# When an evicted PSUM bank counts as free, and which banks the expert layers may use, in a planned attention-and-expert kernel

## The chip, the cores and the metric

One core of one Trainium2 chip runs the program. The metric is the device time of one execution in microseconds, the median over several runs. Profiles come from single executions of the same program; their times are given in microseconds from the start of the span, the first to the last instruction on the core.

## What is computed

Sliding-window causal attention (8 batches, 8 heads, 576 tokens, head size 64, window 64), and behind it one feed-forward expert on all 4608 tokens:

```python
scores = (1 / sqrt(64)) * q @ k.T            # per batch and head
mask = (rel >= 0) & (rel < 64)               # rel = query position - key position
attn = softmax(where(mask, scores, -1e9))
x = (attn @ v) -> [4608, 512]                # heads side by side
h = x @ w_in                                 # 512 -> 2048
g = h * sigmoid(h)                           # silu
out = g @ w_out                              # 2048 -> 512
```

Inputs and outputs are float32; the kernel computes its matmuls in bfloat16 and accumulates in float32.

## The kernel before

**Two kinds of work share TensorE.** *Attention* goes batch by batch. A batch is three units of 192 query tokens. A unit (`add_unit`, from line 486) is one scores step of 48 small matmuls (L331) into four PSUM banks, four exponentials on ScalarE (L337), four mask products on VectorE (L340), one values step of 48 small matmuls (L349) into two banks, and for each of these a reciprocal (L356), a normalisation (L359) and a transpose (L363) into the SBUF tensor `bridge`, which holds the attention output for the expert.

*The expert* (`add_tile`, from line 531) goes over nine tiles of 512 tokens, numbered 0 to 8. The first layer of a tile is 16 groups, one for each 128 hidden columns. A group is four matmuls of 512 columns (L369) that accumulate in one bank; ScalarE evicts the bank with silu into an SBUF tile `g` (L375). The second layer is four output groups of 128 tokens; each is 16 matmuls of 512 columns (L381) into one bank, which ScalarE or VectorE copies to SBUF (L387), and SP stores to HBM (L391). Tiles 0 and 1 are cut into narrower pieces, since their input is only just there; in the last tile the last output group is cut into 256, 128 and 128 columns.

**Eight banks, three pools.** A PSUM bank holds 512 float32 numbers on each partition, one group. Line 177 names the pools: `at`, banks 0 to 3, for scores; `pv`, banks 4 and 5, for values; `mp`, banks 4 to 7, for the expert; and `all`. So values and expert share banks 4 and 5.

**The order is planned ahead.** `Plan.run` (lines 47 to 119) is a list scheduler that runs while the program is built. Every operation has a class, a duration for each engine that can do it, dependencies, a class rank and a *lat*. The planner steps through modelled time and gives each free engine the ready operation of the lowest rank; expert matmuls have rank 99, so attention goes first when it can. Classes are first in, first out, so the expert's matmuls keep their order, and scores may start only while more than 14 second-layer matmuls of the tile are left (`scores_may_run`, line 402). The result is a fixed instruction order for each engine. On the chip the engines wait for each other by semaphores; modelled times have no force there, only the order and the banks.

**When a bank is free, for the planner.** An operation is *seen* at its modelled end plus its *lat* (line 97). A bank is given until an operation that frees it (`untils`): the silu (line 563) or the copy (line 584), and for values the normalisation. It is idle once that operation has been seen (line 75). Among the idle banks, line 80 sorts: for the expert, banks 6 and 7 come ahead of 4 and 5, and within each pair the one seen longest ago. The default *lat* is 0.08 us (line 28). A first-layer matmul is modelled at 0.0036 + columns/2400 us, with *lat* 0.1 (line 555); a silu at 0.18 + columns × 0.00083 us (line 561), and 1.28 more where ScalarE's function table changes (line 93); a copy at 0.18 + columns/1160 us on ScalarE (line 581).

Of the kernel before, what the change touches and what calls it, by code (L numbers as in the profile page):

```python
# [14 lines left out]
class Plan:  # L15
# [31 lines left out]
    def run(self):  # L47
        head = {c: 0 for c in self.queues}
        engines = sorted({e for q in self.queues.values() for op in q for e in op["us"]})
        free = {e: 0.0 for e in engines}  # L50
        can = {e: [c for c, q in self.queues.items() if any(e in op["us"] for op in q)] for e in engines}
        table, left = "exp", self.count
        pipe, sent = {True: 2.0, False: 0.0}, []
        events, order = [0.0], []
        while left:
            if not events:
                raise RuntimeError([(c, head[c], q[head[c]]["n"]) for c, q in self.queues.items() if head[c] < len(q)])
            now = self.now = heapq.heappop(events)
            while events and events[0] == now:
                heapq.heappop(events)  # L60
            moved = True
            while moved:
                moved = False
                for e in engines:
                    if free[e] > now:
                        continue
                    best, kept = None, set()
                    heads = [(self.queues[c][head[c]], c) for c in can[e] if head[c] < len(self.queues[c])]
                    for op, c in sorted(heads, key=lambda x: x[0]["first"]):
                        if e == "POOL" and op["dma"] and len(sent) >= 8 and sent[-8] > now:  # L70
                            continue
                        if e not in op["us"] or not self.done(op["deps"]) or (op["gate"] and not op["gate"]()):
                            continue
                        if op["pool"]:
                            idle = [i for i in self.pools[op["pool"]] if i not in kept and self.done(self.banks[i])]
                            if len(idle) < len(op["untils"]):
                                if op["pool"] != "mp":
                                    kept.update(self.pools[op["pool"]])
                                continue
                            idle.sort(key=lambda i: (op["pool"] == "mp" and i in self.pools["pv"],  # L80
                                                     max([u["seen"] for u in self.banks[i]], default=0.0)))
                            op["bank"] = idle[:len(op["untils"])]
                            for i, until in zip(op["bank"], op["untils"]):
                                self.banks[i] = until
                        best = (op, c)
                        break
                    if best is None:
                        continue
                    op, c = best
                    head[c] += 1  # L90
                    us = op["us"][e]
                    if op["table"] and op["table"] != table:
                        table, us = op["table"], us + 1.28
                    end = free[e] = now + us
                    soft = e == "POOL"
                    if op["dma"] is None:
                        op["seen"] = end + op["lat"]
                    elif soft:

                        begin = max(pipe[True], end + 1.4)  # L100
                        pipe[True] = begin + op["dma"] * (1.5 if pipe[False] > begin else 1.0)
                        op["seen"] = pipe[True] + op["lat"] + 1.2
                        sent.append(op["seen"])
                        heapq.heappush(events, op["seen"])
                    else:
                        begin = max(pipe[False], end + 1.0)
                        busy = pipe[True] > begin
                        pipe[False] = begin + op["dma"] * (1.6 if busy else 1.0)
                        if busy:
                            pipe[True] += 0.6 * op["dma"]  # L110
                        op["seen"] = pipe[False] + {"ld0": 1.2, "st": 1.2}.get(c, 3.0)
                    op["at"], op["cls"], op["by"] = now, c, e
                    order.append((op, e))
                    left -= c != "warm"
                    moved = True
                    heapq.heappush(events, end)
                    heapq.heappush(events, op["seen"])
        for op, e in order:
            op["fn"](e)
# [3 lines left out]
def kernel(ctx, tc, q, k, v, w_in, w_out, out):  # L123
# [244 lines left out]
    def first_layer(bank, j, ft, c, lo, hi):  # L368
        nc.tensor.matmul(  # L369
            banks[bank["bank"][0]][:, 0:hi - lo], lhsT=w_in_sb[:, c, ft * 128:(ft + 1) * 128],  # L370
            rhs=bridge[:, (j * TT + lo) // 64:(j * TT + hi) // 64, c], start=(c == 0), stop=(c == NDC - 1),
        )

    def silu(bank, gt, lo, hi):
        nc.scalar.activation(out=gts[gt][:, lo:hi], in_=banks[bank["bank"][0]][:, 0:hi - lo], func=ACTF.Silu)  # L375
# [4 lines left out]
    def second_layer(bank, gt, m, f, lo, hi):  # L380
        nc.tensor.matmul(  # L381
            banks[bank["bank"][0]][:, 0:hi - lo], lhsT=gts[gt][:, m * 128:(m + 1) * 128], rhs=w_out_sb[:, f, lo:hi],
            start=(f == 0), stop=(f == NFT - 1),
        )

    def copy_out(e, bank, ot, lo, hi):
        copies[e](out=ots[ot][:, lo:hi], in_=banks[bank["bank"][0]][:, 0:hi - lo])  # L387

    def store(ot, j, m, lo, hi):
        r0 = j * TT + m * 128  # L390
        nc.sync.dma_start(out=out[r0:r0 + 128, lo:hi], in_=ots[ot][:, lo:hi])  # L391
# [134 lines left out]
    n_gt, free_gt = [0], {}  # L526
    n_ot, free_ot = [0], {}
# [3 lines left out]
    def add_tile(j):  # L531
# [18 lines left out]
        for i, (ft, lo, hi) in enumerate(work):  # L550
            have = [op for n in range((j * TT + hi + 191) // 192) for op in o_done[n]]
            g, si = gt[ft]
            bank = None
            for c in range(NDC):
                op = p.add("moe", {"PE": 0.0036 + (hi - lo) / 2400}, None,
                           have + win[ft] + (exps[0] if j == 0 else []), lat=0.1,
                           pool=None if c else "mp")
                bank = bank or op
                op["fn"] = lambda _, bank=bank, ft=ft, c=c, lo=lo, hi=hi: first_layer(bank, j, ft, c, lo, hi)
                moe.append((op, 1, 1 if c == 0 and (i == 0 or hi > work[i - 1][2]) else -1))  # L560
            si.append(p.add("silu", {"ACT": 0.18 + (hi - lo) * 0.00083}, lambda _, bank=bank, g=g, lo=lo, hi=hi:
                            silu(bank, g, lo, hi), [op] + free_gt.get(g, []), table="silu"))
            bank["untils"][0] = [si[-1]]
        order = [(m, f, 0, d_model) for m in range(4) for f in range(NFT)]
        if j == 0:
# [3 lines left out]
        bank, uses = {}, {}  # L569
        for i, (m, f, lo, hi) in enumerate(order):  # L570
            g = gt[f][0]
            op = p.add("moe", {"PE": 0.0036 + (hi - lo) / 2400}, None, gt[f][1] + [wout[f // 2]], lat=0.1,
                       pool=None if f else "mp")
            bank.setdefault((m, lo), op)
            op["fn"] = lambda _, bank=bank[(m, lo)], g=g, m=m, f=f, lo=lo, hi=hi: second_layer(bank, g, m, f, lo, hi)
            moe.append((op, 2, len(order) - i))
            uses.setdefault(g, []).append(op)
            if f == NFT - 1:
                ot = n_ot[0] % NOT
                n_ot[0] += 1  # L580
                cp = p.add("out", {"DVE": 0.18 + (hi - lo) / 1000, "ACT": 0.18 + (hi - lo) / 1160},
                           lambda e, bank=bank[(m, lo)], ot=ot, lo=lo, hi=hi: copy_out(e, bank, ot, lo, hi),
                           [op, free_ot.get(ot)])
                bank[(m, lo)]["untils"][0] = [cp]
                free_ot[ot] = p.add("st", {"SP": 0.45}, lambda _, ot=ot, m=m, lo=lo, hi=hi: store(ot, j, m, lo, hi), [cp],
                                    dma=0.75 * (hi - lo) / d_model)
# [7 lines left out]
    def warm(op):  # L594
# [4 lines left out]
                 pool="all")  # L599
    for lo, hi in ((0, 256), (256, 512), (512, 1024), (1024, 1536), (1536, 2048)):  # L600
# [6 lines left out]
          table="silu")  # L607
# [10 lines left out]
    while n_tile < NTT:  # L618
        add_tile(n_tile)
        n_tile += 1  # L620
# [31 lines left out]
```

The softmax here doesn't subtract the row's maximum and nothing guards it: scores larger than these inputs give would overflow.

## Time and profile before

| | |
|---|---|
| median of 5 runs | 299.74 us (299.14 to 301.05) |
| the profiled execution, its own time | 301.05 us |
| its span | 299.2 us |
| expert tiles 2 to 6, with attention in them, each | about 31.2 us |
| tile 7 (240.6 to 268.4), no attention | 27.8 us |
| TensorE / ScalarE / VectorE busy | 96% / 59% / 47% |
| evictions by silu, 512 columns | 0.60 us each |
| copies of an output group, 512 columns | 0.58 us each |
| granted clock of TensorE | full, in all slices |
| last loads from HBM issued | 145.0 to 149.0 us |

The first 84 us hold the loads' start, the first two batches of attention, and tiles 0 and 1. From there the program is regular: a tile's first layer in one stretch, then its second layer with the next batch's three units inside it. The last values step is at 238 us; tiles 7 and 8 run without attention.

How to read it: a matmul's record covers its way through the array, and the next matmul starts before it ends. So a TensorE busy share near 100% does not tell whether matmuls follow each other as densely as they can; the distance between the starts of successive ones does. A weight load (PEld) stands beside each matmul and overlaps it. A row's idle is the time in which that engine did nothing just before it, and behind the arrow stands what released it; "issue" means that the profile shows nothing it waited for.

### The profile page before, as it was taken

The page shows a single profiled execution, that of the slowest core. Times are in us where ns is not written, and L with a number is a line of the kernel's source. Part 1 is how long each engine was busy: PE and PEld are TensorE (multiplying, and loading weights), DVE is VectorE, ACT ScalarE, POOL GpSimd, SP SyncE. Part 2 cuts the span into 40 slices and gives each one's busy share as a digit, 9 for nine tenths or more (in the row PEclk, how much of TensorE's full clock was granted, in tenths as well). Part 3 has the DMA queues.
Part 4 walks back from the last instruction along what each step waited for, and adds up shares of the span by engine and source line. Part 5 has one row for each costly group of instructions (what it writes and reads, how often), then busy time and mean ns, then how long its engine had stood idle before and what let it go on. Part 6 is the DMA issues. An engine that isn't in the chain of part 4 may idle for free.

```text
span 299.2 us, 8484 instructions
## 1 busy us (share of the span) xinstructions
PE 287.0 (96%) x3609; PEld 149.6 (50%) x3641; DVE 139.3 (47%) x340; ACT 176.2 (59%) x340; POOL 117.8 (39%) x175
## 2 busy tenths in 40 slices
PE   8979979899999999999999999999999999999996
PEld 4657634785544544445444544445444544444444
DVE  3882367978886379327941693067006510000000
ACT  4878645886466745675378437752866376126511
POOL 8965995969898989960500000000000000000000
PEclk9999999999999999999999999999999999999999
DMA  8999999999999999992770210011001100110012
GB/s 169 172 175 168 141 169 173 228 142 132 173 172 143 101 180 184 151 100 74 77 75 0 72 39 36 2 37 72 35 0 39 72 35 0 37 71 35 2 70 71
DMA packets 82982, 28.64 MB, mean 96 GB/s; under 512 B 72448, under 2 KB 78208, under 8 KB 82944
## 3 DMA queue, kind: packets, MB, share of 16 engines
q0 software_dynamic: 77184, 18.07, 65.2%
q1 hardware_dynamic: 5760, 10.03, 9.5%
q8 instruction: 28, 0.46, 0.6%
q14 instruction: 10, 0.08, 0.1%
HBM read 36.70 MB, written 9.44 MB: 154 GB/s over the span
## 4 chain that ended last, share of the span: by engine, by line
PE 80%; DMA 8%; POOL 7%; issue 3%; ACT 1%; POOLq 0%; ACTq 0%
PE mp L381 38%; PE mp L369 37%; DMA nat<-in_q_dram 3%; PE mp L349 3%; PE at L331 3%; DMA w_out_sb<-in_moe_w_out_dram 2%; DMA vv<-in_v_dram 2%; POOL vv L253 2%; POOL nat L239 2%; POOL w_out_sb L265 1%; POOL natb L229 1%; POOL w_in_sb L259 1%; ACT ot L387 0%; ACT g L375 0%; PE at L349 0%
## 5 line engine op out<-in xcount | busy, mean ns | idle before, releaser
L369 PE MATMUL mp<-bridge,w_in_sb 128*128 128x512 bf16 (+5 forms) x696 | 128.6, 342 | 2.6 <-ACT g L375 0.8
L381 PE MATMUL mp<-w_out_sb,g 128*128 128x512 bf16 (+2 forms) x576 | 124.4, 367 | 4.5 <-issue 3.2
L375 ACT ACTIVATE g<-mp 128x512 bf16<-128x512 f32 (+5 forms) x174 | 89.6, 523 | 31.4 <-PE mp L369 29.3
L369 PEld LDWEIGHTS <-w_in_sb 128*128 128x128 bf16 x696 | 66.2, 97 | 63.0 <-issue 7.5
L381 PEld LDWEIGHTS <-g 128*128 128x128 bf16 x608 | 56.0, 98 | 62.0 <-issue 1.4
L387 ACT COPY ot<-mp 128x512 f32<-128x512 f32 (+2 forms) x36 | 20.2, 563 | 62.4 <-PE mp L381 43.1
L340 DVE TENSOR_TENSOR e<-e,mask 128x384 bf16<-128x384 bf16 x84 | 26.1, 349 | 49.2 <-ACT e L337 48.7
L337 ACT ACTIVATE e<-at 128x384 bf16<-128x384 f32 x90 | 37.4, 498 | 17.5 <-PE at L331 17.3
L239 POOL DMA_DIRECT2D nat<-in_k_dram x56 | 34.9, 637 | 12.3 <-DMA vv<-in_v_dram 4.3
L253 POOL DMA_DIRECT2D vv<-in_v_dram x32 | 31.9, 1015 | 13.5 <-PE mp L349 12.9
L239 POOL DMA_DIRECT2D nat<-in_q_dram x56 | 34.8, 641 | 3.0 <-DMA w_in_sb<-in_moe_w_in_dram 1.4
L363 DVE STREAM_TRANSPOSE bridge<-ox 128x384 bf16<-128x384 bf16 x48 | 24.8, 553 | 0.0
L246 DVE STREAM_TRANSPOSE qt<-nat 128x576 bf16<-128x576 bf16 x28 | 20.8, 784 | 6.6 <-DMA nat<-in_q_dram 6.6
L246 DVE STREAM_TRANSPOSE kt<-nat 128x576 bf16<-128x576 bf16 x28 | 20.6, 778 | 4.8 <-DMA nat<-in_k_dram 4.8
L359 DVE TENSOR_TENSOR ox<-mp,rc 128x384 bf16<-128x384 f32 x43 | 21.4, 537 | 0.1
L356 DVE RECIPROCAL rc<-mp 128x6 f32<-128x6 f32 x43 | 7.9, 190 | 18.8 <-PE mp L349 18.0
L349 PEld LDWEIGHTS <-e 128*32 128x32 bf16 x1152 | 10.9, 95 | 8.9 <-issue 5.2
L299 DVE COPY vv<-vv 64x576 bf16<-64x576 bf16 (+1 forms) x14 | 7.5, 533 | 13.0 <-DMA vv<-in_v_dram 10.7
L331 PE MATMUL at<-qt,kt 32*128 32x64 bf16 x1008 | 11.9, 190 | 1.0 <-DVE kt L246 1.0
L349 PE MATMUL mp<-vv,e 128*32 128x65 bf16 x1032 | 12.6, 194 | 0.2 <-ACT e L337 0.2
L331 PEld LDWEIGHTS <-kt 32*128 32x128 bf16 x1008 | 9.4, 92 | 5.5 <-issue 3.8
L375 ACT ACT_TABLE_LOAD x7 | 9.0, 1283 | 0.1
(53 smaller groups left out, 85.9 us busy)
## 6 DMA issues: line engine op xcount, KB each, us to landing
out_dram<-ot SPq DMA_DIRECT2D x35, 256.0 KB, 2.1
vv<-in_v_dram POOLq DMA_DIRECT2D x32, 144.0 KB, 5.5
nat<-in_q_dram POOLq DMA_DIRECT2D x56, 72.0 KB, 4.2
nat<-in_k_dram POOLq DMA_DIRECT2D x56, 72.0 KB, 3.9
w_out_sb<-in_moe_w_out_dram POOLq DMA_DIRECT2D x8, 256.0 KB, 6.3
w_in_sb<-in_moe_w_in_dram POOLq DMA_DIRECT2D x6, 256.0 KB, 7.4
w_in_sb<-in_moe_w_in_dram POOLq DMA_DIRECT2D x4, 128.0 KB, 5.4
natb<-in_q_dram POOLq DMA_DIRECT2D x3, 144.0 KB, 4.9
```

Source lines behind the costliest of these rows:

```text
L239: nc.gpsimd.dma_start(out=nats[i][32 * h:32 * h + 32].rearrange("p (m x) -> p m x", m=NB), in_=(q, k)[kk][b, 4 * a + h].rearrange("(m p r) ...
L246: nc.vector.transpose(out=to[:, (2 * a + part) * S:(2 * a + part + 1) * S].rearrange("x (m t r) -> x m r t", t=32, r=2), in_=nats[i].rearr ...
L253: queue[e].dma_start(out=vv[b % NV][:, 2 * g0 + 1:2 * g1 + 1:2, 0:D], in_=v[b].rearrange("h s d -> (h s) d").rearrange("(g p) d -> p g d", ...
L331: nc.tensor.matmul(at_six(op["bank"][h])[:, a, x], lhsT=kt[b % NK][r, at:at + 128], rhs=qt[b % NK][r, at:at + 64], start=(s == a == x == 0 ...
L337: nc.scalar.activation(out=es[n % NE], in_=at_six(bank), func=ACTF.Exp, scale=scale)
L340: nc.vector.tensor_mul(es[n % NE], es[n % NE], mask0 if g == 0 else mask)
L349: nc.tensor.matmul(at_pv(bank)[32 * h:32 * h + 32, x, t], lhsT=e_of(b, a, n, h)[:, x, 32 * t:32 * t + 32], rhs=vv[b % NV][:, (4 * a + h) * ...
L359: nc.vector.tensor_mul(oxs[n % NOX], at_pv(bank)[:, :, :, 0:D], rcs[n % NRC].unsqueeze(3).to_broadcast([128, 3, 2, D]))
L363: nc.vector.transpose(out=bridge[:, n0:n0 + 3, 2 * a:2 * a + 2].rearrange("x t s (u i) -> x t s u i", u=2), in_=oxs[n % NOX].rearrange("p ...
L369: nc.tensor.matmul(banks[bank["bank"][0]][:, 0:hi - lo], lhsT=w_in_sb[:, c, ft * 128:(ft + 1) * 128], rhs=bridge[:, (j * TT + lo) // 64:(j ...
L375: nc.scalar.activation(out=gts[gt][:, lo:hi], in_=banks[bank["bank"][0]][:, 0:hi - lo], func=ACTF.Silu)
L381: nc.tensor.matmul(banks[bank["bank"][0]][:, 0:hi - lo], lhsT=gts[gt][:, m * 128:(m + 1) * 128], rhs=w_out_sb[:, f, lo:hi], start=(f == 0) ...
```

## The change

Two edits in the planner's input, one in its choice of banks.

1. The silu operations and the copies of tiles 2 to 8 (`j > 1`) get *lat* 0.22 in place of 0.08. For the planner their banks come free 0.14 us later, and so do the results that other operations wait for: `g` for the second layer, `ot` for the store.
2. Once the planner has placed the last values step (the queue `pv` is used up), an operation that asks for a bank gets any of the eight in place of its own pool. Only expert groups are left by then. The sort of line 80 stays, so banks 4 and 5 still come last.

No instruction is added or taken away by these lines; what can differ is the bank that a group gets, and through the modelled times the order in which the planner places operations.

```diff
-                            idle = [i for i in self.pools[op["pool"]] if i not in kept and self.done(self.banks[i])]
+                            idle = [i for i in self.pools[op["pool"] if head["pv"] < len(self.queues["pv"]) else "all"] if i not in kept and self.done(self.banks[i])]
                             if len(idle) < len(op["untils"]):
                                 if op["pool"] != "mp":
                                     kept.update(self.pools[op["pool"]])
...
             si.append(p.add("silu", {"ACT": 0.18 + (hi - lo) * 0.00083}, lambda _, bank=bank, g=g, lo=lo, hi=hi:
-                            silu(bank, g, lo, hi), [op] + free_gt.get(g, []), table="silu"))
+                            silu(bank, g, lo, hi), [op] + free_gt.get(g, []), lat=0.22 if j > 1 else 0.08, table="silu"))
             bank["untils"][0] = [si[-1]]
...
                            lambda e, bank=bank[(m, lo)], ot=ot, lo=lo, hi=hi: copy_out(e, bank, ot, lo, hi),
-                           [op, free_ot.get(ot)])
+                           [op, free_ot.get(ot)], lat=0.22 if j > 1 else 0.08)
                 bank[(m, lo)]["untils"][0] = [cp]
```

## The prediction

> **What bounds the kernel now.** I read the page's busy times first, then the groups by line, the chain that ended last, the waits of TensorE after the loads are through, and last the order of time inside one expert tile.
>
> The page:
>
> ```profile
> span 299.2 us, 8484 instructions
> ...
> PE 287.0 (96%) x3609; PEld 149.6 (50%) x3641; DVE 139.3 (47%) x340; ACT 176.2 (59%) x340; POOL 117.8 (39%) x175
> ...
> PEclk9999999999999999999999999999999999999999
> ...
> L369 PE MATMUL mp<-bridge,w_in_sb 128*128 128x512 bf16 (+5 forms) x696 | 128.6, 342 | 2.6 <-ACT g L375 0.8
> L381 PE MATMUL mp<-w_out_sb,g 128*128 128x512 bf16 (+2 forms) x576 | 124.4, 367 | 4.5 <-issue 3.2
> L375 ACT ACTIVATE g<-mp 128x512 bf16<-128x512 f32 (+5 forms) x174 | 89.6, 523 | 31.4 <-PE mp L369 29.3
> ```
>
> TensorE is busy 96% of the span and no other engine passes 59%; the granted clock is full in all 40 slices. The two expert layers, L369 and L381, are the kernel. But 96% hides how densely matmuls follow each other: a 512-column record lasts 0.38 us, and the next one starts long before it ends. So the pitch must be read, and the chain gives it. Its columns are start, length and work; these are the two expert tiles that run after attention:
>
> ```profile
> 240.59 13.99 PE mp L369 x64
> 254.58 0.22 PE mp L381
> ...
> 268.40 14.08 PE mp L369 x64
> 282.48 0.22 PE mp L381
> ```
>
> Both layers have 64 matmuls of 512 columns in such a tile. The second layer takes 268.40 − 254.58 = 13.82 us, 215.9 ns each; the first takes 13.99 and 14.08, so 218.6 and 220.0 ns. The first layer loses 0.17 to 0.26 us a tile, and the second nothing. Where, the waits of the weight loads from 84.5 us on say (total, times, longest):
>
> ```profile
> PEld L369 <- issue: 4.9, 30, 0.2
> ```
>
> and the order of time in one tile shows the place (start, length, then idle before and its releaser):
>
> ```profile
> 247.61 0.60 ACT L375 ACTIVATE g<-mp 128x512 bf16<-128x512 f32 x1 [0.27 <-PE mp L369]
> 248.26 1.61 PEld L369 LDWEIGHTS <-w_in_sb 128*128 128x128 bf16 x8 [0.16 <-issue]
> 248.47 0.60 ACT L375 ACTIVATE g<-mp 128x512 bf16<-128x512 f32 x1 [0.27 <-PE mp L369]
> 249.38 0.60 ACT L375 ACTIVATE g<-mp 128x512 bf16<-128x512 f32 x1 [0.31 <-PE mp L369]
> 250.03 0.96 PEld L369 LDWEIGHTS <-w_in_sb 128*128 128x128 bf16 x5 [0.16 <-issue]
> ```
>
> Two things are to be seen. The gaps come every 250.03 − 248.26 = 1.77 us, eight matmuls or two groups; eight at 215.9 ns take 1.727 us, so one gap costs the matmuls 0.043 us, and the 0.16 us before the weight load (mostly its normal spacing) isn't the loss. And L375 waits for TensorE before each eviction, so ScalarE keeps up; what is late is the bank. From the single records of one such gap: last matmul of a group starts at 250.669, L375 starts 0.475 later, lasts 0.597, and the matmul that re-uses the bank starts at 251.791, 0.050 after that. A bank is held 1.122 us from that last start. Re-used two groups later, it has five pitches, 5 × 0.2158 = 1.079 us: short by 0.043.
>
> **The change, part by part.** Why two banks alternate though the pool has four is in the planner's arithmetic. A group costs 4 × (0.0036 + 512/2400) = 0.868 us there; its bank is free 0.1 + 0.605 + 0.08 = 0.785 after the group's end. That is 0.083 before the next group is through, so bank 6 counts as idle again, and the sort key takes 6 and 7 before 4 and 5. *lat* 0.22 makes it 0.925, which is 0.057 after: a bank of two groups ago is no longer on offer. The planner's hold from the last matmul's start becomes 0.217 + 0.925 = 1.142 against the 1.122 measured.
>
> I walked one tile's sixteen groups by these rules, with the table load (1.28) ahead of the first silu and the previous output group in bank 7. Before: 6 7 4 5 6 7 4 6 7 6 7 6 7 6 7 6. Banks repeat at distance two from the tenth group on, and that is where the matmul records show gaps (10th, 12th, 14th, 16th group of tiles 2 to 7). Tile 8 has no table load to catch up with and shows six. 6 × 4 + 6 = 30, the count above, so the walk can be trusted. After: 6 4 7 5 6 7 4 6 7 5 6 7 4 6 7 5, and the second layer begins on 6. Nothing returns in under three groups, which leaves 9 × 0.2158 = 1.94 us for a hold of 1.122.
>
> *Silu's lat, tiles 2 to 8.* 30 gaps × 0.043 = 1.29 us.
>
> *The copy's lat, tiles 2 to 8.* The second group of a tile today takes the bank of the last output group and starts 0.016 to 0.018 us late in six tiles: 6 × 0.017 = 0.10 us. In the walk it takes bank 4, whose last reader (L359) is through 1.5 us earlier. Between output groups nothing is gained: they are 16 × 0.2159 = 3.45 us apart, and those boundaries show no gap. The store that depends on the copy is issued by SP in the same order; its 2.1 us to landing is hidden but for the last one, which follows the same copy.
>
> *All eight banks.* Binding only after the last values group is planned, at about 238 us: tiles 7 and 8, which rotate over 0 to 3, 6 and 7. Their ten gaps are counted above and the new *lat* alone would remove them, so this part adds 0. Banks 0 to 3 were last read by L337, long before.
>
> *Cost.* No instruction is added; a start that waited for one ScalarE count waits for another. For sharing banks 4 and 5 with the values matmuls (L349) the trace has no row of the new pattern. From below: 0, if the second layer never sits on them when values come, as in the walk. From above: every pair of values and scores (now one block, 103.32 to 104.45 = 1.13 us) is split in two blocks, 0.65 (113.24 to 113.89) plus 0.64 (103.81 to 104.45) = 1.29, so 0.16 for each of ten pairs in five tiles, 1.6 us. I take 0, as the walk reproduced today's gaps exactly.
>
> *A rule against it.* During these 30 gaps the granted clock is 1.00 in every window of the trace. The Trainium skill, TensorE: Matmul & The Clock Gate, "A second HAM failure mode: psum-queue depth-cycling", reports a kernel whose cycling through banks left small idles between groups, and whose clock then swung between half and full. By that rule one first-layer stage at half clock would be an estimated 14 us longer. The trace already has the idles without the swing, so the row decides and I charge nothing.
>
> *Cover.* Saved time must not run into the next wait. From 84.5 us on no matmul waits for a load: batch 3's q and k are transposed by 93.0 and its V shifted by 97.4, against scores at 98.85 and values at 103.32; each later batch is earlier still. At 0.2 us a tile the cover stays. Tiles 0 and 1 keep 0.08, so the first 84 us, where loads bind, are planned as before.
>
> **Sum.** 1.29 + 0.10 = 1.39 us. The profiled execution has 301.05, its span 299.2 and 1.85 around it; it would be 299.66, span 297.8. It is the slowest of five runs; against their median, 299.74 − 1.39 = 298.35, say 298.4.
>
> **Rivals.** *Pairs split.* If a second-layer group takes bank 4 or 5, values must wait for its copy while the scores go ahead. For it: six of a tile's sixteen groups on banks 4 and 5 where there were three. Against: the walk's start on 6. One split per tile: 5 × 0.16 = 0.8 given back, 299.74 − 0.59 = 299.2.
>
> *Slower: values shut out twice.* Tiles 3 and 4 begin with two units of the batch that runs inside the tile before (those after need one). The second unit's transposes end at 110.91, the next tile starts at 115.83: 4.9 us of slack. One second-layer group in the way costs 3.45 + 0.58 + about 0.3 of hand-over = 4.3, which fits. With two (8.6) TensorE stands still 3.7 us ahead of each of these two tiles: 299.74 − 1.39 + 7.4 = 305.8. It decides only beyond 4.9 us. Against: in the walk the output groups find 6 and 7 free in turn.
>
> *It does nothing.* If the order inside the plan leaves only the bank of two groups ago idle, the gaps stay: 299.7. For: four banks, two of them shared. Against: in today's walk 4 and 5 are idle at each of those groups and are passed over only for the sort key.
>
> **How the numbers follow.** Forecast 0.82, pairs split 0.07, slower 0.05, nothing 0.06. Half a per cent, about what a measurement of this kernel can tell from no change, is 1.50 us, and 1.39 is just short; the runs shown lie 299.14 to 301.05, so two medians may differ by some 0.4 without cause. About half of the forecast's chance falls beyond the bound: faster 0.42, same 0.52 (the rest of it, the splits, the nothing), slower 0.06. The range runs from the full gain plus that scatter, 297.7, to nothing gained, 299.6.
>
> **What would show it.** Right: chain pieces of L369 at 13.81 us instead of 13.99 to 14.08; the line of 30 idles of its weight loads gone; L375's idle before each eviction an even 0.27 instead of 0.27 and 0.31 in turn; L349 and L331 still following each other directly; clock full. Wrong: L349 standing apart from L331, an idle before L369 put down to DVE, gaps of 0.16 left in first-layer stretches, or a change before 84 us.

## The result, and the profile after

The changed kernel takes 298.86 us (median of 27 runs, 297.72 to 301.95) against 300.09 us (53 runs) of the kernel before: a ratio of 0.9958, 95% interval 0.9945 to 0.9972. That is 1.26 us, with 0.84 to 1.65 inside the interval.

The page of the profiled execution, whose own time is 299.00 us:

```profile
span 297.2 us, 8483 instructions
...
PE 284.9 (96%) x3609; PEld 149.6 (50%) x3641; DVE 138.9 (47%) x340; ACT 176.3 (59%) x340; POOL 117.4 (39%) x175
...
PEclk9999999999999999999999999999999999999999
...
L369 PE MATMUL mp<-bridge,w_in_sb 128*128 128x512 bf16 (+5 forms) x608 | 108.9, 337 | 3.3 <-DMA w_in_sb<-in_moe_w_in_dram 1.3
...
L369 PE MATMUL at<-bridge,w_in_sb 128*128 128x512 bf16 x88 | 20.0, 379 | 0.0
```

The shares are those of before, the clock is full, and a new row shows first-layer matmuls that write banks 0 to 3 (*at*). The busy share is still 96%, so it says nothing about a gain; the chain does (start, length, work). Four consecutive first layers, the last in pieces because its banks belong to two pools:

```profile
146.14 13.81 PE mp L369 x64
...
177.12 13.81 PE mp L369 x64
...
208.08 13.81 PE mp L369 x64
...
239.03 3.45 PE at L369 x16
242.49 1.73 PE mp L369 x8
244.21 3.45 PE at L369 x16
247.67 1.73 PE mp L369 x8
249.39 3.45 PE at L369 x16
```

A first layer takes 13.81 us, 64 × 215.8 ns, the pitch that only the second layer had. The waits of the weight loads after 84.5 us have no row of L369 left; before, it headed them with 30 idles. In tile 7 the order of time (start, length, then idle before and its releaser) reads:

```profile
246.04 0.60 ACT L375 ACTIVATE g<-at 128x512 bf16<-128x512 f32 x1 [0.27 <-PE at L369]
246.90 0.60 ACT L375 ACTIVATE g<-at 128x512 bf16<-128x512 f32 x1 [0.27 <-PE at L369]
...
249.49 0.60 ACT L375 ACTIVATE g<-mp 128x512 bf16<-128x512 f32 x1 [0.27 <-PE mp L369]
```

The evictions are as long as before, 0.60 us, and come at an even 0.27 us of idle: ScalarE now runs at TensorE's beat, where 0.27 and 0.31 alternated.

Attention's steps keep their order. In tile 3's second layer a values step (L349) is followed directly by the next scores step (L331), as before:

```profile
128.97 0.48 PE at L331 x48
...
133.44 0.49 PE mp L349 x40
133.93 0.48 PE at L331 x48
134.41 0.16 issue
134.57 3.83 PE mp L381 x17
```

The 0.16 us of "issue" behind such a pair is not idle time: it is the place of a matmul that has no record. This profile, like the one of the kernel before, has 576 matmul records of L381 beside 608 weight loads; the profiles of four programs below (each part alone, and longest idle first) have 608 of both and no such piece, and the next recorded matmul starts 0.13 us behind the step's last one and not 0.35, about one pitch sooner.

**Where the two microseconds of span are.** The span is 2.0 us shorter, more than the runs show, so it has to be cut in two. The stretch from the first matmul of tile 2 to the last matmul of the kernel fell from 211.445 to 210.116 us: 1.33 us. The rest, 84.71 − 84.03 = 0.68 us, lies ahead of tile 2 (three batches of attention, 0 to 2, and not two, are done there, with tiles 0 and 1), where both programs have the same TensorE instructions on the same banks. The other programs below show what that part is worth: in the eight of them that share this beginning, tile 2 starts anywhere from 83.21 to 84.92 us. A single profile's span can't resolve a change of 1.3 us here; the stretch can.

### The profile page after: what moved, and what is told of

Same layout as the page of the kernel before. It is cut to its first block, busy times and chain, and to the rows that moved or that the text cites. A ratio compares the mean times of both kernels' runs of the same rounds, so it can differ in the third digit from the quotient of the medians.

```text
span 297.2 us, 8483 instructions
## 1 busy us (share of the span) xinstructions
PE 284.9 (96%) x3609; PEld 149.6 (50%) x3641; DVE 138.9 (47%) x340; ACT 176.3 (59%) x340; POOL 117.4 (39%) x175
## 4 chain that ended last, share of the span: by engine, by line
PE 82%; POOL 8%; DMA 5%; issue 3%; ACT 1%; POOLq 0%; ACTq 0%
PE mp L381 33%; PE mp L369 30%; PE at L369 6%; PE at L381 6%; DMA w_in_sb<-in_moe_w_in_dram 3%; PE at L331 3%; PE mp L349 3%; POOL w_in_sb L259 2%; POOL nat L239 2%; POOL vv L253 2%; DMA w_out_sb<-in_moe_w_out_dram 2%; POOL natb L229 1%; POOL w_out_sb L265 1%; ACT ot L387 0%; ACT g L375 0%
## 5 line engine op out<-in xcount | busy, mean ns | idle before, releaser
L369 PE MATMUL mp<-bridge,w_in_sb 128*128 128x512 bf16 (+5 forms) x608 | 108.9, 337 | 3.3 <-DMA w_in_sb<-in_moe_w_in_dram 1.3
L381 PE MATMUL mp<-w_out_sb,g 128*128 128x512 bf16 (+1 forms) x482 | 105.3, 368 | 4.7 <-issue 3.2
L369 PEld LDWEIGHTS <-w_in_sb 128*128 128x128 bf16 x696 | 66.6, 98 | 62.1 <-issue 2.7
L375 ACT ACTIVATE g<-mp 128x512 bf16<-128x512 f32 (+5 forms) x152 | 76.6, 513 | 26.2 <-PE mp L369 25.0
L381 PEld LDWEIGHTS <-g 128*128 128x128 bf16 x608 | 56.0, 98 | 62.1 <-issue 1.4
L387 ACT COPY ot<-mp 128x512 f32<-128x512 f32 (+1 forms) x30 | 16.9, 565 | 46.6 <-PE mp L381 27.4
L369 PE MATMUL at<-bridge,w_in_sb 128*128 128x512 bf16 x88 | 20.0, 379 | 0.0
L381 PE MATMUL at<-w_out_sb,g 128*128 128x512 bf16 (+1 forms) x94 | 19.2, 361 | 0.1
L375 ACT ACTIVATE g<-at 128x512 bf16<-128x512 f32 x22 | 12.9, 597 | 4.5 <-PE at L369 4.5
L349 PEld LDWEIGHTS <-e 128*32 128x32 bf16 x1152 | 10.9, 95 | 9.1 <-issue 5.4
L349 PE MATMUL mp<-vv,e 128*32 128x65 bf16 x1032 | 12.7, 194 | 0.3 <-ACT e L337 0.2
```

Of the source, the lines that this page charges most:

```text
L349: nc.tensor.matmul(at_pv(bank)[32 * h:32 * h + 32, x, t], lhsT=e_of(b, a, n, h)[:, x, 32 * t:32 * t + 32], rhs=vv[b % NV][:, (4 * a + h) * ...
L369: nc.tensor.matmul(banks[bank["bank"][0]][:, 0:hi - lo], lhsT=w_in_sb[:, c, ft * 128:(ft + 1) * 128], rhs=bridge[:, (j * TT + lo) // 64:(j ...
L381: nc.tensor.matmul(banks[bank["bank"][0]][:, 0:hi - lo], lhsT=gts[gt][:, m * 128:(m + 1) * 128], rhs=w_out_sb[:, f, lo:hi], start=(f == 0) ...
```

## The experiments

All changes of time below are of that stretch, from one profile each, read from the starts of single matmul records (the program that prefers banks 4 and 5 begins tile 2 in another order and is compared tile by tile). Where no ratio to the kernel before is given, the program ran once. The single records also give each gap: the start of a matmul less the start of the one before, less 215.8 ns.

| program | stretch, us | against before |
|---|---|---|
| before | 211.445 | |
| the whole change | 210.116 | −1.329 |
| silu's lat alone | 210.195 | −1.250 |
| copy's lat alone | 211.343 | −0.102 |
| eight banks alone | 210.982 | −0.463 |
| longest idle first | 210.538 | −0.907 |
| lat 0.15 | 211.387 | −0.058 |
| lat 0.18 | 210.094 | −1.351 |
| two banks after attention | 211.987 | +0.542 |
| silu of 448 columns | 210.177 | −1.268 |
| silu of 480 columns | 210.625 | −0.820 |
| lat 0.22 in all tiles | 210.120 | −1.325 |

### One part at a time

Silu's *lat* alone:

```diff
-                            silu(bank, g, lo, hi), [op] + free_gt.get(g, []), table="silu"))
+                            silu(bank, g, lo, hi), [op] + free_gt.get(g, []), lat=0.22 if j > 1 else 0.08, table="silu"))
```

> Only the silu operations of tiles 2 to 8 get lat 0.22; the copies keep 0.08 and the pools stay apart. Theory (the gain is the 30 late banks of the first layer): all 30 go, the small late starts of the second group (0.017 us, six tiles) stay, so the stretch from tile 2's first layer to the end is 1.29 us shorter than before and 0.10 longer than with the whole change; first-layer pieces of 13.82 to 13.84 us; ratio to before near 0.9957. Rival (the deeper pool after attention carries the gain): tiles 7 and 8 keep their ten gaps, 13.99 and 14.08 us, and at most 0.86 us is gained.

Measured: 1.250 us off the stretch; ratio 0.9959 (0.9944 to 0.9974). All 30 gaps are gone, the six late second groups stay at 0.017 us, and tiles 7 and 8 are as short as the others without any of the banks 0 to 3. The deeper pool doesn't carry the gain.

The copy's *lat* alone:

```diff
-                           [op, free_ot.get(ot)])
+                           [op, free_ot.get(ot)], lat=0.22 if j > 1 else 0.08)
```

> Only the copies of tiles 2 to 8 get lat 0.22. Theory: the 30 gaps of 0.043 us stay (in tile 8 one group earlier than before), the six small late starts go, 0.10 us gained from tile 2 on; first-layer pieces of 13.97 to 14.08 us. Rival (the copy holds up the second layer or the next tile): 0.5 us or more gained, and second-layer stretches shorter.

Measured: 0.102 us off the stretch, 30 gaps left (in tile 8 at the same groups as before, not one earlier), first-layer pieces of 13.98 and 14.06 us; the six late starts are gone. That the sum agrees to 0.002 us is luck: two profiles of this bank sequence differ by 0.044 (the next section).

Eight banks alone:

```diff
-                            idle = [i for i in self.pools[op["pool"]] if i not in kept and self.done(self.banks[i])]
+                            idle = [i for i in self.pools[op["pool"] if head["pv"] < len(self.queues["pv"]) else "all"] if i not in kept and self.done(self.banks[i])]
```

> Only the eight-bank pool after attention; lat stays 0.08. Theory: the 20 gaps of tiles 2 to 6 stay and the ten of tiles 7 and 8 go with two small late starts, 0.46 us gained from tile 2 on; first-layer pieces of 13.99 us in tiles 3 to 6 and 13.81 in tiles 7 and 8; ratio near 0.9985. Rival (eight banks are what matters): 1.3 us, ratio 0.9957.

Measured: 0.463 us off the stretch; ratio 0.9983 (0.9962 to 1.0004). The waits of this run's weight loads from 84.5 us on (total, times, longest):

```profile
PEld L369 <- issue: 3.3, 20, 0.2
```

20 of 30 are left, those of tiles 2 to 6. The silu's part and the copy's add up to 1.352 us, within 0.023 of the whole; the eight banks save what the new *lat* would save anyway in tiles 7 and 8, and add nothing to it.

### How large must lat be

The same two lines with 0.15 and with 0.18 in place of 0.22, pools as before.

> lat 0.15 in place of 0.22 for silu and copy of tiles 2 to 8, pools apart as before. In the planner's numbers a bank is then free 0.855 us after its group and the next group ends after 0.868, so the bank of two groups ago is still on offer. Theory (a threshold in the planner at 0.163): the 30 gaps stay, only the six small late starts go; 0.10 us gained from tile 2 on. Rival (the gain grows with lat): half of it, some 0.65 us, is gained.

> lat 0.18, pools apart as before. Theory (threshold at 0.163): 0.885 against 0.868, so no bank comes back in under three groups; all 30 gaps and the six small ones gone, the stretch from tile 2 on as short as with the whole change within 0.05 us, 1.34 us under before; the eight-bank pool is worth nothing on top. Rival (0.22 is needed since the measured hold is 1.122): gaps of some 0.04 us are left in tiles 2 to 8.

Measured: with 0.15 all 30 gaps stay (13.98 and 14.07 us a piece) and 0.058 us is gained; with 0.18 none is left (13.81 us a piece) and 1.351 us is gained, ratio 0.9960 (0.9942 to 0.9979). 0.03 us of *lat* decides it all, and 0.18, with which the planner's hold is 0.217 + 0.885 = 1.102 us and so short of the measured 1.122, does as well as 0.22. So *lat* is a switch here: once the bank of two groups ago isn't offered, the next one is of three groups ago, with over 0.8 us to spare. The 0.15 program has the bank sequence of the copy's *lat* alone, and its six late starts are gone too, so it should have gained the same 0.102; the 0.044 between the two is scatter, for which no record shows a cause.

### The hold itself

These two keep the banks and the order of before and make the eviction shorter. The silu leaves out the last 64 or 32 columns of tiles 2 to 8:

```diff
-                            silu(bank, g, lo, hi), [op] + free_gt.get(g, []), table="silu"))
+                            silu(bank, g, lo, hi if j < 2 else 448), [op] + free_gt.get(g, []), table="silu"))
```

> The kernel before, with its banks and its order; only the silu of tiles 2 to 8 evicts 448 of its 512 columns, so the last 64 tokens of each tile keep older values of g (left out: that part of the activation). Theory (a gap is the measured hold, 1.122 us, less the 1.079 there is): the eviction gets some 0.053 shorter (64 columns at 0.83 ns), the hold falls to 1.069, under 1.079, and the 30 gaps vanish though banks 6 and 7 still alternate; 1.3 us gained from tile 2 on. Rival (re-use of a bank after two groups costs something of its own, whatever the hold): the 30 gaps of 0.043 stay.

> As the run with 448, but 480 of 512 columns are evicted (the last 32 tokens of each tile are left out of the activation). Theory: eviction 0.027 shorter, hold 1.095, gaps of 0.016 us, so some 0.8 us gained from tile 2 on. Rival: gaps stay at 0.043.

Measured: at 448 columns the eviction takes 0.544 us and no gap is left, 1.268 us off the stretch; at 480 it takes 0.571 and the 30 gaps are 0.017 us each (expected 0.016), 0.820 us off. The order of time at 480, then at 448, in tile 7:

```profile
248.17 0.57 ACT L375 ACTIVATE g<-mp 128x480 bf16<-128x480 f32 x1 [0.29 <-PE mp L369]
249.04 0.57 ACT L375 ACTIVATE g<-mp 128x480 bf16<-128x480 f32 x1 [0.31 <-PE mp L369]
```

```profile
248.14 0.54 ACT L375 ACTIVATE g<-mp 128x448 bf16<-128x448 f32 x1 [0.32 <-PE mp L369]
249.01 0.54 ACT L375 ACTIVATE g<-mp 128x448 bf16<-128x448 f32 x1 [0.32 <-PE mp L369]
```

The two idles are nearer to each other at 480 columns, 0.29 and 0.31, and even at 448, with the same two banks in turn. So re-using a bank after two groups costs nothing in itself; it costs the hold beyond five pitches, and 0.053 us of eviction was all that stood between the old order and none of the 30 gaps (the six late second groups stay). The same sum says why only every second group is late: the 0.043 us by which one group starts late is added to the five pitches of the next one's bank, and 1.079 + 0.043 is the hold of 1.122.

### Two banks

The whole change, with banks 6 and 7 alone after attention:

```diff
-        {"at": range(4), "pv": range(4, 6), "mp": range(4, 8), "all": range(8)},
+        {"at": range(4), "pv": range(4, 6), "mp": range(4, 8), "all": range(8), "two": range(6, 8)},
...
-                            idle = [i for i in self.pools[op["pool"] if head["pv"] < len(self.queues["pv"]) else "all"] if i not in kept and self.done(self.banks[i])]
+                            idle = [i for i in self.pools[op["pool"] if head["pv"] < len(self.queues["pv"]) else "two"] if i not in kept and self.done(self.banks[i])]
```

> The whole change, but after attention the expert has only banks 6 and 7. Theory (a bank is held 1.122 us from its last matmul's start, and the other banks cover ScalarE's table load at a tile's start): tile 7's third group waits 1.06 us for the silu behind the table load, then six gaps of 0.043, so its first layer takes 15.1 us; tile 8 alternates from the start, seven gaps, 14.13 us; 1.65 us longer from tile 2 on than the whole change. Rival (two banks are enough, the gaps were something else): both pieces stay at 13.81 to 13.85 us.

Measured: 1.871 us longer than the whole change, where 1.65 was expected. Tile 7's first layer takes 15.13 us, as expected: its third group starts 1.05 us late, and six gaps follow. The start of that tile in order of time:

```profile
239.91 1.28 ACT L375 ACT_TABLE_LOAD   x1
...
241.21 1.08 ACT L375 ACTIVATE g<-mp 128x512 bf16<-128x512 f32 x2
241.85 3.44 PE L369 MATMUL mp<-bridge,w_in_sb 128*128 128x512 bf16 x15 [0.89 <-ACT g L375]
```

ScalarE loads its function table for 1.28 us, the first silu comes only then, and TensorE's third group has no bank. Here the wait is in the open, with its releaser, unlike the 0.043 us gaps. So the third and fourth banks cover the table load, and two would do elsewhere but for the 0.043. Tile 8's piece is 14.36 us and not 14.13. It has six gaps and not the seven expected, but its second group starts 0.296 us late, when the last copy of tile 7 ends, where 0.017 was expected. That copy starts 0.740 us after the start of tile 7's last matmul, against 0.460 in the kernel before: ScalarE's wait for that matmul ends at the same distance in both, 0.420, and the copy follows 0.32 us later and not 0.04. The profile puts these 0.32 us under "issue", so what held the copy stays open. The clock did not: the granted clock is 1.00 through tiles 7 and 8, and the half clock that lowers this run's mean to 0.999 begins 2.5 us after the kernel's last matmul.

### The rival with values shut out

Two programs let output groups land on banks 4 and 5. In the first, the kernel before takes the bank that has been idle longest; in the second, the changed kernel prefers 4 and 5.

```diff
-                            idle.sort(key=lambda i: (op["pool"] == "mp" and i in self.pools["pv"],
+                            idle.sort(key=lambda i: (False,
                                                      max([u["seen"] for u in self.banks[i]], default=0.0)))
```

> The kernel before, but the sort takes the bank that has been idle longest among 4 to 7, without preferring 6 and 7; lat stays 0.08. Theory (any order that does not hand back the bank of two groups ago removes the gaps): no gap of 0.043 us in tiles 2 to 8, 1.3 us gained there; but the first output group of tiles 3 and 5 lands on bank 4 or 5, values are planned after all three scores steps in these two tiles, and two more switches a tile cost 4 x 0.16 = 0.64 us. Net 0.65 to 0.75 us from tile 2 on, ratio near 0.9977. Rival (the modelled hold itself matters, not the order of banks): gaps stay in some tiles and less than 0.3 us is gained.

```diff
-                            idle.sort(key=lambda i: (op["pool"] == "mp" and i in self.pools["pv"],
+                            idle.sort(key=lambda i: (op["pool"] == "mp" and i not in self.pools["pv"],
                                                      max([u["seen"] for u in self.banks[i]], default=0.0)))
```

> The whole change, but the sort prefers banks 4 and 5 for the expert, the banks that values need. Theory: no gap in the first layers, but output groups sit on 4 and 5, all three scores steps of a tile come ahead of its values, and each of tiles 2 to 6 has two more switches: 5 x 2 x 0.16 = 1.6 us longer from tile 2 on than the whole change, the upper price of the prediction; the second unit's values move from 30 to 17 matmuls ahead of the next tile, 2.8 of the 4.9 us of slack, so no first layer waits. Rival (values shut out stall the next tile): TensorE idle of 1 us or more ahead of L369 with a VectorE releaser, 4 us or more lost.

Measured, longest idle first: no gap of 0.043 us, 0.907 us off the stretch, more than the 0.65 to 0.75 expected; ratio 0.9966 (0.9951 to 0.9982). Tiles 3 and 5 last 31.18 and 31.17 us from first layer to first layer, against 30.98 and 30.96 with the whole change. The chain of tile 3's second layer in this run:

```profile
128.50 0.48 PE at L331 x48
128.98 3.99 PE mp L381 x18
132.97 0.48 PE at L331 x48
133.45 2.70 PE mp L381 x12
136.15 0.51 PE at L331 x48
136.66 1.83 PE mp L381 x8
138.49 0.49 PE mp L349 x42
138.97 2.05 PE mp L381 x9
141.02 0.48 PE mp L349 x42
141.51 3.78 PE mp L381 x17
145.29 0.49 PE mp L349 x48
```

Three scores steps (L331) and then three values steps (L349), each by itself. The planner gives the second output group bank 5 in tile 3 and bank 4 in tile 5 (the second, not the first as expected), so values come only after its copy, behind 38 matmuls of the layer (18, 12 and 8 above) and not 18, and the pairs of before are split. That is the picture of the rival *Pairs split*. Its price is 0.20 us a tile, 0.10 a split, not the 0.16 that was expected.

Preferring 4 and 5: ratio to before 0.9990 (0.9975 to 1.0005), so most of the gain is given back. The first output group of each of tiles 2 to 6 is on bank 4, the second on 5. Tiles 3 to 6 have the same split order and last 0.21 us longer each than with the whole change, where 0.32 was expected (two splits at 0.16); the beginning differs too, with a values step inside tile 2's first layer. But no first layer waits: from 110 us on the only idle of TensorE's matmuls that the profile lists is the 0.2 us behind attention's steps, the place of the missing records. With two output groups on the values' banks the second unit's values start 4.75 us ahead of tiles 3 and 4 and not 7.6, and its transposes end 2.1 us ahead and not 4.9. So two groups in the way delay it by 2.9 us, where the slower rival reckoned 8.6: the first unit's values come 5.3 us later, and as all scores are done by then, the second's follow them after 2.5 us and not 5.0. A delay beyond the slack of 4.9 us, which that rival needs, occurs in neither program, and one that makes it wasn't tried.

### The early tiles

The whole change with *lat* 0.22 in tiles 0 and 1 too (`lat=0.22` in both lines).

> The whole change with lat 0.22 for tiles 0 and 1 too. Theory (before tile 2 the expert waits for loads and for ScalarE, not for a bank of two groups ago: all first-layer gaps there sum to under 0.08 us): the stretch from tile 2 on is as short as with the whole change within 0.05 us, and the start isn't shorter; ratio to before 0.9945 to 0.9975. Rival (the early tiles lose banks as well, and the change left that untouched): another 0.3 us or more, ratio under 0.9945.

Measured: ratio 0.9961 (0.9944 to 0.9978), stretch 210.120 us, tile 2 starts at 84.22. The stretch is as expected and no gain is seen ahead of it, but a start that varies by 1.7 us from profile to profile can't show a few tenths, and the interval reaches just to the rival's 0.9945. No program run beats the changed kernel by more than the intervals are wide; the silu's *lat* alone and 0.18 in both lines equal it.

## Why the prediction was right

It stated 298.4 us in 297.7 to 299.6; the median is 298.86. In its own terms, 1.39 us was forecast and 1.33 is measured in the stretch, 1.26 in the ratio. The kernel before, run 53 times, has a median of 300.09 and not the 299.74 of the five runs shown, which is most of the remaining 0.46.

- **30 gaps × 0.043 = 1.29:** measured 1.250 by the silu's *lat* alone.
- **Six late second groups × 0.017 = 0.10:** measured 0.102 by the copy's *lat* alone, nearer than two profiles agree; that the six late starts are gone is what shows the term.
- **All eight banks add 0:** by itself 0.463, on top of the rest nothing (210.094 us with pools apart and *lat* 0.18, 210.116 with the whole change).
- **The threshold:** free 0.785 us after a group against 0.868. *lat* 0.15 and 0.18 lie on either side of 0.163 and decide all 30 gaps.
- **The hold of 1.122 against 1.079:** shown by the shorter evictions, 0.017 at 480 columns and nothing at 448.
- **The bank sequence** after the change is the walked one for tiles 3 to 6, with 6 and 7, and 4 and 5, changing roles; in tile 2, which still follows a copy with the old *lat*, the first groups differ. The second layer begins on a bank of the pair 6 and 7, so the values keep theirs.
- **The upper price of sharing, 0.16 for each split pair,** was mis-sized: 0.10. It was read from chain pieces that each end in 0.16 us of "issue", and a split adds one such piece. These 0.16 us are the place of a matmul without a record (576 records of L381 for 608 weight loads), not a cost. By the starts of single records in one of the runs with all records (longest idle first), a values-and-scores pair puts the next matmul off by 1.06 us, and the two steps apart by 0.58 each, 1.16 together. The forecast took the other end, so nothing in its sum hung on it; the 299.2 of *Pairs split* and what was expected of the last two bank orders did.
- **The slower rival's 8.6 us** for two output groups in the way was too much: 2.9 with both groups on the values' banks.
- **The clock rule** of the Trainium skill, TensorE: Matmul & The Clock Gate, "A second HAM failure mode: psum-queue depth-cycling", was set aside because the old gaps left the clock at 1.00. The granted clock is 1.00 with the change too, with six banks in rotation in tiles 7 and 8.
- **Chances:** a change within half a per cent had 0.52, and 0.42% it was. That the gain lies just short of that bound was said; its interval reaches across it, so on which side it fell is in part luck.

## What to carry to other kernels

In a plan of modelled times, look for the decision that sits on an edge: a lag that was 0.08 us too short cost 0.043 us thirty times, because it put a bank back on offer just before it was free, and a preference then took it each time. Count such losses by the distance between starts, per group, and against a layer that runs clean; the idle a profile prints next to the gap can be four times the loss, and the busy share doesn't move at all. Beyond the edge the exact lag did not matter here (0.18 and 0.22 gave the same time), but which banks the other work needs did. And count the records before reading an idle as a cost: where a matmul has none, the profile prints its place as idle.

## What the runs showed of the hardware

- The chain from matmul to matmul through an eviction is steady to a few ns in the 24 late groups of tiles 2 to 7 of the kernel before: 0.475 us from the last matmul's start to the eviction's, 0.597 us for 512 columns (0.571 for 480, 0.544 for 448 in the other two programs, so 0.83 ns a column), 0.050 us to the next matmul.
- Changing between 512-column matmuls and a step of small ones costs TensorE time by itself: between the starts of single records, 0.31 us into a step (0.09 over the pitch of 215.8 ns), 0.12 to 0.13 us out of it, and 0.13 from a values step to a scores step.
- The scatter between profiles sits mostly in the first 84 us: tile 2 starts 1.7 us apart in ten programs with the same beginning. Behind it the three programs without any gap took 210.094, 210.116 and 210.120 us.
